# A new hand-over order for 1,900 pieces of an attention and gating kernel, with three more groups of idle products

## The chip, the cores and the metric

The kernel runs on one core of a Trainium2 chip. The metric is device time in microseconds (us), the median of several executions; lower is better. The engines are TensorE (PE in the rows, with its weight loads as PEld), VectorE (DVE), ScalarE (ACT), GpSimd (POOL) and SyncE (SP), which here only issues DMAs.

## The reference

Windowed attention with four sink keys, and behind it a gated feed-forward layer whose gate mixes positions:

```python
# q, k, v: (4, 8, 768, 64) f32; n_sink 4, window 128
scores = scale * np.matmul(q, k.transpose(0, 1, 3, 2))
keep = is_sink | in_window                     # 4 first keys, or the last 128
a = np.exp(scores - max); a = a / (sum + 1e-9)
x = (a @ v) as (4, 768, 512)
h = np.maximum(x @ w_in, 0.0)                  # w_in (512, 1024)
u, v = h[..., :512], h[..., 512:]
v_n = (v - mean) / np.sqrt(var + 1e-06)
v_s = np.einsum('ts,bsd->btd', w_spatial, v_n) + b_spatial[None, :, None]
return (u * v_s) @ w_out                       # (4, 768, 512)
```

## The kernel before

The work is cut into about 1,900 pieces. A batch b has six tiles t of 128 positions, and each tile two halves hf of four heads; the 48 halves are numbered 0 to 47. For one half there are these pieces:

- `scores`: products of queries and keys into banks `sc` (L882 in f32 in the first batch, L888 as three f16 products later). VectorE then adds the mask and takes the maximum (L893, out `pexp` and `nm`), ScalarE takes the exponential (L898).
- `weights`: `pexp` is split into a high and a low f16 part (`p`; high is L538 on ScalarE or L547 on GpSimd, low is L554 on VectorE or GpSimd), and SyncE issues two DMAs that transpose them into `pT` (L963). In the first three tiles of batch 0 TensorE transposes instead (`weights_whole`, L930 and L945 into `tr`), and ScalarE or VectorE copies `tr` to `pT` (L934, L948).
- `attend`: `pT` times values into `av` (L1001 to L1003 with the sinks in L995; in the first three tiles L1014 with the sinks in L1009). VectorE divides by the sum (L1021 to L1025), two engines split the result into `x`, and a DMA transposes it to `xT` (L1045).

Behind these stand the large products, all of them through `three` (L575), each a sum of three f16 products: `ps_v` (half v of `x @ w_in`, 12 products of 512 columns), `ps_u` (half u, 12 of 256), `ps_s` (the mix over positions, 18 of 256) and `ps_o` (the output, 12 of 512). Loading and splitting the weights (`decode`, L634 to L641, then L540 and L561) is also cut into pieces, which stand between those of the first batches. L638 is one of its steps on VectorE, and L561 the low part of a split.

There are few buffers: four banks `sc`, one double bank `av`, and two banks `mm` that `tr`, `ps_v`, `ps_u`, `ps_s`, `ps_o` and the idle products share.

What is emitted, and in which order, is one table of numbers, `ORDER`. A number is a piece by its rank; a letter behind it (a, d, p) names the engine where a piece may run on several. Each engine's queue is this table read from the start, so each engine runs its pieces in that order and waits where one's inputs or buffer are not there:

```python
    def order(self):
        self.prepare()
        todo = [(self.ps[int(x.rstrip("adp"))], x[-1]) for x in ORDER]
        todo = [(p, e if e in "adp" else p[2]) for p, e in todo]
        self.where = {p[1]: e for p, e in todo}
        for p, e in todo:
            yield p[4], e
```

A piece is registered with a time and a number `columns`, which describe it to whoever makes the table; `order` reads neither.

`keep_clock` (L1174) makes one group of idle products: four products of ones with 256 columns into a bank that nobody reads. `FILLERS` says how many such pieces exist; those that `ORDER` names are emitted. Before, it names six of 24.

Of the kernel before, what the change touches and what calls it, by code (L numbers as in the profile page):

```python
# [19 lines left out]
P = 128  # L20
# [247 lines left out]
FILLERS, FILLER = 24, 4  # L268
# [3 lines left out]
5 0 1895 1 3 2 4 1908 6 11 1898 10 53 1889 7 164 1894 9 14 13 8 42 39 15 44 16 43 51 41 40 50 62 46 47 45 63 37 1887 64 17 112 48 52 116 38 111 73 19  # L272
229 74 12 65 49 68 105 67a 21 72 20 18 69 83 66 82 22 387 54 71 75 70 88 86 91 55 85 87 25 26 104 89d 100 84 172 163 101 107 162 23 92 103 61 93 128
106 31 319 110 263 109 108 246 27 32 123 90 129 113 102 28 57 115a 132 459 114a 127 131 209 165 126 124a 194 141 156 142 140 143 33 130 29 146 125 34
150 159 222 151 139 158 183 221 94 154 145a 147 144a 133 166 152 148 182 153 96 169a 173 135 35 155 179 157 161 178 171 76 193 170a 36 160 188 30 95
223 185 168 192 186 199 97 197a 187 190 174a 191 205 24 215 206 175 184 58 230 207p 118 201 228 189 198 217 149 220 78 212p 98 200 210 243 196d 204
219 218 225 216 56 244 224 59 211 232 134 117 213 245a 226 257 119 208 250 77 252p 233 227 248 176 247 260 234a 259 276 251 240 136 231 275 239 253
262 167 261 267 120 291 235 283 137 271 277a 258 274 138 79 236 270 121 286 343 279 285 288 278 280 344 305 60 287 99 304 292 177 313 281d 346 294
306a 284 122 282 237 297 311p 300 309 299 318 315 307 80 316 293 317 328 327 351p 310 321 298 81 290 337 312 295a 352 289 379 349 323 417 416 353 339
453 329p 340 334 296 372 389 322 326 333p 331 241 342 314 341 302 371 301 330 336 375 350 373a 242 338 332 376 418 335 525 354 264 345 308 355 180  # L280
377p 374 423 424a 366 362 363 360 348 480 383 432 272p 378 385 361 356a 181 249 390 386 358 481 642 357 303 384 421 195 397 347 420 202p 393 394 214
414 320 203p 381 415 392 254 391 398a 422 410 412 238 411 400p 359 413 524 494 419 441a 426 273p 364 430 428a 533 429 365 367 255 475 324a 256 565 409
431 325p 368 438 437 493 577 388 600 265 439 443d 405 594 442 266 506 447 460 444 831 446 268 399 425 395a 448 621 396p 445 507 473a 512 427 531 625
369 497 513 720 269 370 676 440 454 502 727 532 449 488 433 539a 673 435 496 474p 450 582 434 504a 436 540p 689 505 456 461 458 451 541 500p 590 601
465 455 463 406 556 501 467 401 490 495 572 457 602 557 466 1023 603d 498 468 575 610a 573 476a 469 452 574d 464 477 478d 566p 470 492 658 402 462 479
611d 576 499 489 592a 753 471 491 548 593p 659 660d 482 671a 520a 672p 622 549 484 483 550p 825 522d 472 485 407 521 526 560a 563 503 623 562 523 624d
706 567 561p 635a 486 631 510 487 529 636p 637 732 707 509 708p 511 528 514 530 718p 515 686 516 568 380 733 719p 508 734d 517 527 534 745a 687 542a
564 640p 551 638 537 643 755 536 518 746p 905 559 543 688p 519 695a 781 682 554 756 696p 952 535 757d 546p 544 553 538 632 583 569 552 782 555 666 584
717 783d 408 604 854 585a 545 633 1395 587 578 570a 589p 586 760 579 403 580 767a 581 596 547 571 675 598 588 800p 597 612p 684 605 614 777 599 665
609 648 644 646p 607 591 641 613p 617 608 628 639 630 714 759 674 618 606 790 615a 404 683 558 627 647 629 595 1396 768d 663p 619d 649 721 616 626  # L290
669p 873 620 656 657 680 655 667 681 654 780 634 679 690 664 776 668 652 796p 650a 694 670 882 651 678 794 645 700p 699 791 691 692 702 713 834 693
864 870 715 703 704d 710 653 722 835 711 677 661 712 836p 740 747 735 729 662 705 797 738a 844p 728 709 795 701 749 742p 743 731 778 730 752 739 716
751 758 784 741 801d 798 750 744 811 871 764 1071 935 763 876 723a 874p 845d 926 789 779 799 770a 761 725 724 786 812 769 772 792 867 813p 855 773 762
822p 774d 726 802 748 788 787 807 824 736 771 816a 685 737 827 785 823d 775 833 872 818 820p 866 793 927 978 697a 809 803a 808 819 899 810 698p 821
804 837 888 875 889 933p 856 850 830 839 930 817 838 754 805 840 765p 841 829 928 846 828 861 847p 897 766d 860 1111 863 849p 877 806 826 862 814 1842
894p 859 858 883 815 931 885 951 886 991 896p 884 985 869 891 907 848 382 934 878a 865 997 960 911 895 909 1105 868 902 879 901 1029 903 898 908 880
904 932 925 915p 832 887 914 922 910 842a 958 917d 994 1060 881 843p 924 892 992 936 1006 893 921 923 943 1061 900 993 939 947a 918 941 906 995a 944
912p 942 956 948 949d 955 1069p 961 916 940 919 1066 945 1350 950 965 1067 946 1050 962 954 996 920 1336 957 959 1149 890 963 1054 966p 1072 964 981
929 913p 982 1102 1156 1068 937a 969p 1254 1011 938 984 967d 968 971 1118 998 1062 1019 1840 953 972 973d 975 983 1351 1070 1014p 1009 1016 851 1374
1007 1027 1010 970 980 1017 852 1008 1176 976 1051 988 1025 974 977p 1028 1026 989p 999d 1143 1015 1018p 1004 1330 1052 1146 1053d 990d 1064a 1219 986  # L300
853 1065p 1020 1046 1034 1000 1044a 857 1087 1393 1077 987 1005 1075p 1036 1037 1057 1048p 1038 1058 1024 1088 1089d 1184 1035 1100a 1012 1059 1101p
1056 1047 1076 1092a 1049 1001 1185 1150 1186d 1098p 1279 1045 1073 1078 1002 1096 1196a 1055 1003d 1182 1375 1197p 1086 1097 1030 1110 1083 1021p
1093 1085 1107 1022p 1084 1109 1063 1013 1099 1161 1031 1079a 1449 1032d 1043 1074 1039a 1108 1040d 1119 1162 1131 1129a 1080 1263 1163p 1121 1299
1128 1225p 1122 1123 1226 1174a 1140 1106 1264 1141 1227 1132 1120 1175p 1142 1138 1130 1265d 1838 1305 1033 1273p 1115 1133d 1041p 1139 1283 1223
1293 1274d 1169 1167a 1151 1042p 1116 1220 1145 1168 1094 1450 1117p 1170 1152a 1160 1171p 1134 1158 1124a 1157 1179 1153 1181 1328 1095 1159 1103
1144 1125p 1280 1173 1549 1224 1281 1303p 1178 1112 1359 1187 1104 1260 1180 1210 1198 1513 1191 1300 1228 1199p 1193 1387 1190 979 1218 1203p 1201
1177 1363 1192 1154 1211 1216 1212d 1217 1304 1329 1229p 1202 1221 1215 1204 1230p 1247 1214 1245a 1514 1302 1155 1222 1200 1249p 1366a 1165 1231
# [125 lines left out]
def fast_path(tc, st, scalars, qk, v, v0, vs, w_in, w_sp, w_rows, b_sp, b_col, w_out, out):  # L433
# [7 lines left out]
    with (  # L441
# [373 lines left out]
        def whole(b):  # L815
            return b < WHOLE
# [101 lines left out]
        def weights_whole(i, b, t, hf, r):  # L918

            n = n_blocks(t)  # L920
# [16 lines left out]
            if t > 1:  # L937
                k = n // 4
# [348 lines left out]
```

## Time and profile before

| what | us |
|---|---|
| three executions | 400.57, 401.19, 404.01 |
| median | 401.19 |
| the profiled execution, its own time | 399.68 |
| its span, first to last instruction | 397.9 |

The profile describes one execution. Its span is 1.8 us shorter than its time, and its time is 1.5 us under the median of the three. A row of the timeline gives the start, the duration, the engine, the line and the tiles (out<-in) of a run of like instructions; since products overlap in the pipeline, a run's duration reaches a little into the next one. The granted clock (PEclk) is 1.00 at TensorE's 2.4 GHz and 0.50 at 1.2 GHz.

### The profile page before, as it was taken

To read this page: it belongs to the slowest core of one execution; us is meant where nothing else is said; L and a number is where in the kernel's file an instruction comes from. 1 tells how busy PE (TensorE), PEld (TensorE's weight loads), DVE (VectorE), ACT (ScalarE), POOL (GpSimd) and SP (SyncE) were. 2 spreads that over 40 slices of the span, in tenths; PEclk is the share of its full clock that TensorE was granted. 3 is DMA by queue.
4 is the path that set the end of the run, shared out by engine and by line. 5 is a ranking of instruction groups with operands and counts; after the bars stand their busy time and mean duration, and the time that the engine had idled before them with its cause. 6 is when DMAs were issued, how large, how long until landed. Compare 5 with 4: busy or idle time off the path is not lost. (4 is left out here: it accounts for less than half of the span.)

```text
span 397.9 us, 10018 instructions
## 1 busy us (share of the span) xinstructions
PE 386.9 (97%) x3663; PEld 272.1 (68%) x3663; DVE 305.2 (77%) x900; ACT 280.3 (70%) x682; POOL 201.0 (51%) x262
## 2 busy tenths in 40 slices
PE   7998999989999999999999999999999999999995
PEld 5677477667856776567885765686778665678742
DVE  4898799898979998699899789787787757435520
ACT  4997799978988888879889867787775543322111
POOL 5236389665976657365859634634573022113010
PEclk9896899999999999999999999999999999999999
DMA  7998799987899998999999967968658984312003
GB/s 252 390 354 177 192 152 213 259 207 187 162 221 219 215 197 176 215 239 188 195 202 263 220 171 160 232 133 204 105 113 164 172 214 113 126 55 105 28 29 111
DMA packets 134872, 72.91 MB, mean 183 GB/s; under 512 B 114208, under 2 KB 118304, under 8 KB 134816
## 3 DMA queue, kind: packets, MB, share of 16 engines
q1 hardware_dynamic: 134400, 71.94, 79.1%
q8 instruction: 30, 0.49, 0.5%
q10 hardware_dynamic: 416, 0.26, 0.2%
q14 instruction: 26, 0.21, 0.2%
HBM read 38.17 MB, written 6.29 MB: 112 GB/s over the span
## 5 line engine op out<-in xcount | busy, mean ns | idle before, releaser
L575 PE MATMUL ps_s<-wsp,vn 128*128 128x256 f16 x864 | 99.1, 273 | 0.0
L898 ACT ACTIVATE pexp<-pexp,nm 128x260 f32<-128x260 f32 (+1 forms) x192 | 87.1, 486 | 13.0 <-DVE nm L893 12.5
L575 PEld LDWEIGHTS <-vn 128*128 128x128 f16 x864 | 83.1, 98 | 12.0 <-issue 1.7
L575 PE MATMUL ps_u<-xT,win 128*128 128x256 f16 x576 | 68.7, 273 | 0.1
L575 PE MATMUL ps_v<-win,xT 128*128 128x512 f16 x288 | 67.5, 386 | 0.1
L575 PE MATMUL ps_o<-wout,g 128*128 128x512 f16 x288 | 65.2, 379 | 0.4 <-DVE found L757 0.4
L575 PEld LDWEIGHTS <-win 128*128 128x128 f16 x576 | 54.9, 98 | 10.5 <-issue 1.2
L554 POOL TENSOR_TENSOR p<-pexp,p 128x1024 f16<-128x1024 f32 (+1 forms) x23 | 45.4, 1974 | 14.5 <-ACT p L538 13.9
L575 PEld LDWEIGHTS <-xT 128*128 128x128 f16 x288 | 27.8, 99 | 32.3 <-issue 3.1
L575 PEld LDWEIGHTS <-g 128*128 128x128 f16 x288 | 27.6, 98 | 32.2 <-issue 1.8
L554 DVE TENSOR_TENSOR p<-pexp,p 128x16 f16<-128x16 f32 (+2 forms) x49 | 31.4, 644 | 4.6 <-POOL p L547 3.0
L1165 ACT ACTIVATE ob<-ps_o 128x512 f32<-128x512 f32 x24 | 14.2, 592 | 28.9 <-PE ps_o L575 26.9
L1001 PE MATMUL av<-vring,pT 128*128 128x65 f16 x312 | 32.6, 193 | 1.3 <-DMA pT<-p 1.3
L538 ACT CAST p<-pexp 128x32 f16<-128x32 f32 (+2 forms) x54 | 29.6, 563 | 4.2 <-DMA pT<-p 4.0
L547 POOL TENSOR_SCALAR p<-pexp 128x1024 f16<-128x1024 f32 (+1 forms) x18 | 20.1, 1118 | 24.6 <-ACT pexp L898 9.0
L1002 PE MATMUL av<-vring,pT 128*128 128x65 f16 x312 | 32.5, 193 | 0.0
L1003 PE MATMUL av<-vring,pT 128*128 128x65 f16 x312 | 32.4, 193 | 0.1
L1001 PEld LDWEIGHTS <-pT 128*128 128x128 f16 x312 | 28.7, 97 | 3.1 <-DMA pT<-p 1.6
L554 POOL TENSOR_TENSOR g<-g,g 128x256 f16<-128x256 f32 x27 | 20.8, 772 | 18.9 <-ACT g L538 18.2
L1081 POOL TENSOR_SCALAR rs<-mv 128x1 f32<-128x1 f32 x24 | 8.6, 359 | 41.9 <-DVE mv L1074 39.5
L888 PE MATMUL sc<-kring,qp 64*128 64x260 f16 (+1 forms) x432 | 28.9, 262 | 0.6 <-DVE nm L893 0.5
L1139 DVE SCALAR_TENSOR_TENSOR ps_s<-ps_s,b_bc 128x256 f32<-128x256 f32 x35 | 15.1, 430 | 18.4 <-PE ps_s L575 17.1
(155 smaller groups left out, 766.7 us busy)
## 6 DMA issues: line engine op xcount, KB each, us to landing
qkraw<-qk_t SPq DMA_DIRECT2D x18, 512.0 KB, 4.4
out<-ob SPq DMA_DIRECT2D x24, 256.0 KB, 2.9
vraw<-v_s SPq DMA_DIRECT2D x21, 256.0 KB, 4.5
dec<-w_in SPq DMA_DIRECT2D x8, 512.0 KB, 7.0
wrow<-w_in SPq DMA_DIRECT2D x8, 512.0 KB, 3.9
wrow<-w_sp_rows SPq DMA_DIRECT2D x6, 384.0 KB, 3.8
dec<-w_out SPq DMA_DIRECT2D x4, 512.0 KB, 4.6
wrow<-w_out SPq DMA_DIRECT2D x4, 512.0 KB, 3.7
```

The lines of the kernel that those rows point to most:

```text
L538: nc.scalar.copy(o, x)
L547: nc.gpsimd.tensor_scalar(o, x, 1.0 if sc is None else sc, 1.0, op0=ALU.mult, op1=ALU.mult)
L554: eng[e].tensor_tensor(out=o, in0=x, in1=hi, op=ALU.subtract)
L575: nc.tensor.matmul(o, a, m, start=(i == 0), stop=(i == n - 1))
L888: nc.tensor.matmul(o, qp[rows, qi, hp, :], keys(kring[:, ki], rows), start=(m == 0), stop=(m == 2))
L898: nc.scalar.activation(po, po, AF.Exp, bias=nm()[:, h2 + q:h2 + q + 1], scale=-1.0)
L1001: nc.tensor.matmul(o[:, h], ph, vh, start=(t < 2 and j == 0), stop=False)
L1002: nc.tensor.matmul(o[:, h], ph, vl, start=False, stop=False)
L1003: nc.tensor.matmul(o[:, h], pl, vh, start=False, stop=(j == nb - 1 and (t < 2 or h == HH - 1)))
L1081: nc.gpsimd.tensor_scalar(rs, vals["mv", i][:, 1:2], 1e-6, VNS ** -2, op0=ALU.add, op1=ALU.mult)
L1139: nc.vector.scalar_tensor_tensor(out=sums_at(), in0=ps(), scalar=1.0 / (SP_SCALE * VNS), in1=b_bc[:, t0:t0 + TC], op0=ALU.mult, op1=ALU.add)
L1165: plan.add(r + WHEN["o copy"], "a", 0.5, lambda e: nc.scalar.activation(tl("ob", i), tl("ps_o", i), AF.Copy, scale=1.0 / (G_SCALE * OUT_SC ...
```

## The change

`ORDER` is a new table: the same pieces in another order, 133 of them on another engine (30 from GpSimd to ScalarE, 24 the other way; 38 from GpSimd to VectorE, 29 the other way; 12 between ScalarE and VectorE), and nine idle groups instead of six. `FILLERS` rises to 36. The numbers `columns` of the scores, the transposes, the attend products and the idle products are others; `order` does not read them. Nothing that is computed changes.

```diff
-FILLERS, FILLER = 24, 4
+FILLERS, FILLER = 36, 4
...
-5 0 1895 1 3 2 4 1908 6 11 1898 10 53 1889 7 164 1894 9 14 13 8 42 39 15 44 16 43 51 41 40 50 62 46 47 45 63 37 1887 64 17 112 48 52 116 38 111 73 19
...
+5 3 1904 1 0 2 4 1911 11 10 1890 53 6 1903 9 165 1893 8 13 14 1912 111 37 39 15 116 42 40 1909 16 41 45 43 44 46 62 50 47 51 63 164 229 17 49 112 68
...
-                     columns=n * (260 if t else 128) * (2 if whole(b) else 1.5))
+                     columns=n * (260 if t else 128) * (1.2 if whole(b) else 0.8))
...
-                plan.add(r, "PE", 0.44, turn, [("pexp", i, h) for h in hs], [("tr", (i, k))], columns=1024)
+                plan.add(r, "PE", 0.44, turn, [("pexp", i, h) for h in hs], [("tr", (i, k))], columns=1650)
...
-                         columns=4 * 65 * n + (520 if t > 1 else 0))
+                         columns=333 * n + (90 if t > 1 else 0))
...
-                         columns=195 * n + (195 if t > 1 else 0))
+                         columns=165 * n + (30 if t > 1 else 0))
...
-            plan.add(200.0, "PE", 0.01 + 0.108 * FILLER, f, [], [("idle", k)], columns=2 * P * FILLER)
+            plan.add(200.0, "PE", 0.01 + 0.108 * FILLER, f, [], [("idle", k)], columns=2.5 * P * FILLER)
```

Where the three added groups stand: before the first scores there are six instead of five; the one behind all four scores of the first tile now stands between their two halves; a new one stands behind the first two scores of the second tile's second half; and a new one stands between the two last f32 attend products. That last place is on TensorE, in the third tile of batch 0. Before (`sc` are scores of the fourth and fifth tile, `psink` the sink weights):

```order
L882 MATMUL sc<-wsp,qkraw 128x260 x2
L945 MATMUL tr<-ident,psink 16x128
L882 MATMUL sc<-wsp,qkraw 128x260 x2
L930 MATMUL tr<-ident,pexp 128x128 x4
L1009 MATMUL av<-vsraw,pT 128x260
L1014 MATMUL av<-vring,pT 128x65 x8
L1009 MATMUL av<-vsraw,pT 128x260
L1014 MATMUL av<-vring,pT 128x65 x8
L882 MATMUL sc<-wsp,qkraw 128x260 x4
```

Now (four pairs of a weight load and an idle product, of which one stands):

```order
L930 MATMUL tr<-ident,pexp 128x128 x4
L882 MATMUL sc<-wsp,qkraw 128x260 x4
L930 MATMUL tr<-ident,pexp 128x128 x4
L1009 MATMUL av<-vsraw,pT 128x260
L1014 MATMUL av<-vring,pT 128x65 x8
L1174 LDWEIGHTS any
L1174 MATMUL idle<-any 128x256
...
L1009 MATMUL av<-vsraw,pT 128x260
L1014 MATMUL av<-vring,pT 128x65 x8
L882 MATMUL sc<-wsp,qkraw 128x260 x4
```

The idle group came between the two attend products, and the sink transpose (L945) went ahead of the scores.

The second attend product there reads a `pT` that VectorE copies (L934). On VectorE, ahead of that copy, before (L893 is the mask, printed as ISA):

```order
L893 ISA nm 128x1
L638 SCALAR_TENSOR_TENSOR w_487<-dec,w_487 128x512
L893 ISA pexp,nm<-sc,m_odd 128x260
L893 ISA nm 128x1
L934 COPY pT<-tr 128x512
```

Now:

```order
L561 SCALAR_TENSOR_TENSOR vring<-vring 128x8x64
L554 TENSOR_TENSOR x_529<-av,x_529 128x512
L634 TENSOR_SCALAR w_547<-dec 128x512
L561 SCALAR_TENSOR_TENSOR win<-w_322,win 128x512
L561 SCALAR_TENSOR_TENSOR vring<-vraw,vring 128x8x64
L934 COPY pT<-tr 128x512
```

The weight step L638 and the masks ahead of the copy went behind it, and two low parts (L561) came ahead of it.

On SyncE's queue, the four transposes of batch 1's first tile (`p_0` is half 0, `p_1` half 1), which the attend products of that tile wait for. Before:

```order
L963 DMA_TRANSPOSE pT<-p_0_137 128x4x128
L569 DMA qkraw<-qk_t 128x2x512
L569 DMA vraw<-v_s 128x512
L569 DMA vsraw<-v_sink 96x260
L963 DMA_TRANSPOSE pT<-p_1_138 128x4x128
L569 DMA vraw<-v_s 128x512
L963 DMA_TRANSPOSE pT<-p_0_137 128x4x128
L963 DMA_TRANSPOSE pT<-p_1_138 128x4x128
```

Now:

```order
L963 DMA_TRANSPOSE pT<-p_0_137 128x4x128
L569 DMA qkraw<-qk_t 128x2x512
L963 DMA_TRANSPOSE pT<-p_1_138 128x4x128
L963 DMA_TRANSPOSE pT<-p_0_137 128x4x128
L963 DMA_TRANSPOSE pT<-p_1_138 128x4x128
```

Three loads that stood among the four went elsewhere.

## Rows read from the trace of the kernel before

**Rows 1.** The page: TensorE's busy share, and its clock in 40 slices.

```profile
PE 386.9 (97%) x3663; PEld 272.1 (68%) x3663; DVE 305.2 (77%) x900; ACT 280.3 (70%) x682; POOL 201.0 (51%) x262
PEclk9896899999999999999999999999999999999999
```

**Rows 2.** Busy time by stretch; last three columns PEclk, DMA share, GB/s.

```profile
9.20:12.50 3.30, 3.29 (x15) 2.12 (x14) 2.42 (x10) 3.24 (x11) 1.17 (x2) 0.50 1.01 350
12.60:32.90 20.30, 20.30 (x146) 14.95 (x144) 19.04 (x62) 18.91 (x43) 8.49 (x13) 1.00 0.98 351
33.10:43.20 10.10, 9.08 (x33) 5.92 (x34) 7.68 (x25) 8.63 (x18) 6.32 (x6) 0.50 0.86 166
43.30:90.90 47.60, 46.06 (x491) 32.64 (x490) 43.38 (x119) 41.26 (x105) 30.16 (x36) 1.00 0.97 207
90.90:393.20 302.30, 301.13 (x2945) 211.47 (x2942) 228.85 (x665) 203.69 (x500) 148.71 (x179) 1.00 0.77 167
```

**Rows 3.** Waits of TensorE: waited for, us in total, times, longest.

```profile
PE av L1001 <- DMA pT<-p: 1.3, 1, 1.3
PE av L1014 <- DVE pT L934: 1.2, 1, 1.2
PE sc L888 <- DVE nm L893: 0.5, 1, 0.5
```

**Rows 4.** Timeline of TensorE around 33 us.

```profile
30.31 2.00 PE L1014 MATMUL av<-vring,pT 128*128 128x65 f32 x16
32.24 0.70 PE L1009 MATMUL av<-vsraw,pT 16*128 16x260 f32 x2
34.12 3.68 PE L1014 MATMUL av<-vring,pT 128*128 128x65 f32 x16 [1.18 <-DVE pT L934]
37.73 2.10 PE L882 MATMUL sc<-wsp,qkraw 64*128 64x260 f32 x8
39.76 4.47 PE L575 MATMUL ps_v<-win,xT 128*128 128x512 f16 x12
44.17 1.15 PE L882 MATMUL sc<-wsp,qkraw 64*128 64x260 f32 x8
```

**Rows 5.** Timelines of VectorE and GpSimd at the same place.

```profile
30.60 2.52 DVE L638 SCALAR_TENSOR_TENSOR w<-dec,w 128x512 int32<-128x512 int32 x1
33.38 0.68 DVE L934 COPY pT<-tr 128x512 f32<-128x512 f32 x1
35.92 0.69 DVE L638 SCALAR_TENSOR_TENSOR w<-dec,w 128x512 int32<-128x512 int32 x1
...
30.51 2.05 POOL L554 TENSOR_TENSOR p<-pexp,p 128x1024 f16<-128x1024 f32 x1
```

**Rows 6.** Timeline of TensorE in the opening.

```profile
8.66 0.62 PE L1174 MATMUL idle<-any 128*128 128x256 bf16 x4
9.10 1.02 PE L930 MATMUL tr<-ident,pexp 128*128 128x128 f32 x4
10.14 2.10 PE L882 MATMUL sc<-wsp,qkraw 64*128 64x260 f32 x8
...
14.94 0.61 PE L930 MATMUL tr<-ident,pexp 128*128 128x128 f32 x4
```

**Rows 7.** Timelines of TensorE and SyncE at 72 to 80 us; a transpose's landing.

```profile
74.90 2.76 PE L575 MATMUL ps_v<-win,xT 128*128 128x512 f16 x12
78.91 0.84 PE L888 MATMUL sc<-kring,qp 64*128 64x260 f16 x12
...
72.31 1.21 SPq L963 DMA_TRANSPOSE pT<-p  x1
77.11 3.28 SPq L963 DMA_TRANSPOSE pT<-p  x2
...
DMA to landing us min/median/max: 4.7/5.3/5.5
```

More of the change, by code (lines that the diff above doesn't have):

```diff
@@ L276 @@
[L276 to L295, printed above, removed]
@@ new lines @@
+564 576 611p 658 510 491 482 494 592p 483 508 484 562 548 659 472 485 660d 406 631 511 671a 600 593d 520a 622 672d 495 407 521 522p 486 549 509 594
+550d 526 623 560a 515 624d 534 561p 523 583 635a 706 529 636p 538 527 905 567 530 642 528 487 584 555 686 544 637 707 514 708d 676 643 516 718p 638
+551 687 542a 517 688d 732 535 719d 543 568 536 546p 537 553 559 569 1395 518 695a 755 733 554 545 552 734p 580 547 696d 587 570a 745p 578 585a 519
+746p 958 781 756 598 586 579 596 589p 757d 640a 581 666 597 782 1396 588 404 599 591 783d 1105 604 408 767a 612p 854 605 615a 571 850 768p 760 682 609
@@ new lines @@
+994 944 1066 943 941 916 929 939 955 843p 954 1006 950 937d 893 956 938 1449 996 961 1182 940 948 987 1050 957 964 1067 969p 962 1146 963 919 945 971
+981 972 1068 946 1054 953 920 993 983 1149 970 982 906 965 912a 959 1102 984 973d 968 1156 1016 966a 913d 998 974 1118 967p 852 980 1014a 1010 1072
+1008 1011 1007 1069a 1015 1018p 988 1026 1176 975 1009 1028 1070 1393 1025 1336 1019 1330 1219 1034 1027 976 1017 999a 1004 977d 1020 1077 1035 1044p
+1036 1056 1038 1150 890 853 1075p 1000 1073 1037 1087 1043 1048d 1057 1058 1005 1076 1046 989a 1024 1047 1840 1088 990d 1089p 1051 1074 1023 1100p
@@ new lines @@
+1322 1410d 1421 1388 1373 1337 1435 1482 1409 1380 1418 1352 1606 1839 1444 1407 1381 1445 1286 1189 1343a 1453p 1394 1411 1353 1344p 1447 1516 1403a
+1446 1464 1404d 1457p 1455 1417 1465 1607 1466 1386 1467 1454 1206 1509 1473 1425 1608 1605 1521 1486p 1397 1456 1488 1602 1318 1609 1490p 1477 1658
+1476 1501 1459 1474 1436a 1424 1616 1500 1405 1519p 1587 1599 1475 1326 1437 1650 1498 1510 1499 1485 1726 1531 1588 1517 1589d 1540 1489 1841 1659
+1603p 1518 1296 1604p 1660 1532 1541 1533d 1536a 1512 1544p 1504 1545p 1412 1316 1520 1522 1413 1463 1414p 1529 1527 1557 1426p 1621 1530 1491 1555
@@ new lines @@
+1678 1645 1681 1767d 1590 1830 1772 1773 1769 1831 1774 1775 1770 1777 1591 1779d 1814 1778 1780d 1592 1791 1593 1822 1698 1800 1792 1748 1804 1699
+1700 1747 1757 1787 1756 1759 1870 1788 1789d 1793a 1794d 1875 1871 1872d 1873a 1874d 1865 1876 1877d 1878a 1879d 1854 1866 1867d 1868a 1869d 1801
+1855 1856d 1859a 1860d 1781 1802 1803d 1805a 1806d 1795 1782 1783d 1784p 1785p 1825 1796 1797d 1798a 1799d 1819 1826 1827d 1828p 1829d 1807 1820 1701
+1821p 1850 1823a 1832 1808 1824p 1809d 1812p 1813p 1810 1833 1834d 1851 1835a 1836d 1852 1815 1853 1881 1817 1760 1880 1883 1811 1882 1884 1885 1857
@@ L331 @@
+1816 1818 1858 1861 1863 1862 1864
 """.split()
```

79 lines of the change are left out of this document (41 added, 38 removed).

## The prediction

> **What bounds the kernel now.** I read the page first: TensorE is busy for 97% of the span, the other engines for 51 to 77% [rows 1]. The reader should see that no order can gain much by overlapping better; only three things can give: time in which TensorE waits, time in which it runs slow, and the ends of the program. The clock line of the same page shows where it runs slow: two dips in the first 45 us, then nothing below 9 tenths [rows 1]. The stretches by window tell the rest [rows 2]: the clock is 0.50 from 9.2 to 12.5 us and from 33.1 to 43.2 us, 1.00 in between and after 43.3. From 90.9 us to the end of the products, TensorE is busy 301.13 of 302.30 us, so nothing of size is left there. The waits by releaser agree [rows 3]: apart from the start, TensorE waits 1.3, 1.2 and 0.5 us at three places.
>
> The second dip is the dear one. TensorE waits 1.18 us at 33 us for a copy on VectorE, after a stretch of thin f32 attend products, and then runs at 1.2 GHz until 43.2 us [rows 4]. In that dip VectorE is busy 7.68 and ScalarE 8.63 of 10.10 us, so TensorE is what everything waits for. In the first dip ScalarE is busy 3.24 of 3.30 us [rows 2]: there the slow clock costs next to nothing.
>
> **The change part by part.** The numbers in `columns` reach nothing on the chip, since `order` does not read them; neither does a larger `FILLERS`. What changes is the table: an order, engines, and 12 more idle products. All sums are made against the profiled execution, 399.68 us.
>
> The clock from 33 to 43 us. The same work stands in the trace at both levels. Sixteen attend products take 3.68 us there and 2.00 just before; eight scores 2.10 and, at 44.17 us, 1.15 [rows 4]; twelve `ps_v` products 4.47 and, later, 2.76 [rows 4, 7]. If the clock holds, 1.68 + 0.95 + 1.71 = 4.34 us go. Will it hold? Before the fall came thin products and a wait. Now four dense idle products stand in just that place, and the wait should shrink (next paragraph). The same thin products ran at 1.00 from 12.6 to 32.9 us with nothing between them but scores and transposes [rows 2]. I take it that it holds, at 2 in 3; the bounds are 0 and 4.34.
>
> The wait of 1.18 us. It ends with the copy L934 at 33.38 us, which was late because the weight step ahead of it on VectorE took 2.52 us where its sister took 0.69; GpSimd's subtraction ran from 30.51 to 32.56 in the same time [rows 5]. Now that step stands behind the copy. But two low parts stand ahead of it, which also read two tiles, and the same subtraction comes on GpSimd when ScalarE has made the high part; that cast moved from GpSimd to ScalarE, just ahead of ScalarE's own transpose copy. If the low parts run first, the wait goes; if one meets the subtraction, it loses up to 2.52 − 0.69 = 1.8 us again. Between 0 and 1.8 us of wait I take 0.3, as the last low part needs a cast that ScalarE runs ahead of the one that frees the subtraction: −0.9 us.
>
> The Trainium skill (SBUF — State Buffer, section on two separate sides) says that a VectorE operation with two SBUF inputs and a GpSimd operation that reads SBUF take a shared port pair as an exclusive lock: whoever starts first keeps it for its whole instruction. The 2.52 us in this trace agree with it. By that rule it is the start order of the last low part and the subtraction that decides, which is the first rival below.
>
> The idle groups. One takes 0.44 us of the queue in the trace, from its start at 8.66 us to the next start at 9.10 [rows 6]. The sixth one ahead of the first scores lies in the wait for the first data. The one in the second tile lies in a stretch where ScalarE sets the pace (18.91 of 20.30 us busy, [rows 2]): at most 0.5, I take 0.1. The one between the attend products lies in the wait if there is one, else on the path: 0 to 0.5, I take 0.4. Together +0.5. Without cover it is +1.1.
>
> The first dip. Transposes took 1.02 and scores 2.10 there against 0.61 and 1.15 [rows 4, 6], 1.4 us. With ScalarE at 98% of that stretch I count it at 0 (bounds 0 and −1.4).
>
> The wait at 81 us, 1.3 us [rows 3]. `av` of batch 1 waits for a transposed `p`. The third and fourth transposes were issued at 77.11 us, 4.8 us behind the first, and land some 5.3 us later [rows 7]. Now three of the four loads between them are gone. Twelve scores (0.84 us, [rows 7]) that stood in front of the wait went further ahead, so TensorE also comes earlier. Bounds 0 and −1.3; I take −0.6.
>
> The feeders. If TensorE gains some 5 us at 33 to 43 us, VectorE and ScalarE must deliver everything after that so much earlier. From 33.1 to 90.9 us VectorE is busy 7.68 + 43.38 of 57.7 us, idle 6.6; ScalarE 8.63 + 41.26, idle 7.8 [rows 2]. Gains of 5.5 us would leave VectorE 1 us idle in 52, a share of 98%, and ScalarE would need 96%. VectorE reached 94% from 12.6 to 32.9 us (19.04 of 20.30), so I expect part of it back: 0 to +3.5, I take +1.5. What hides it is that the table puts other `ps_u` products ahead there.
>
> Engines. 133 pieces move, net 15 away from GpSimd, mostly high parts to ScalarE. Nothing after 90.9 us waits for them, since TensorE is never short there [rows 2]; the 0.5 us wait of a score [rows 3] may go or turn up elsewhere: 0. The order of large products among themselves costs nothing: each kind takes the same wherever it stands, and scores are entered from another kind as often as before.
>
> Sum: −4.3 − 0.9 + 0.5 − 0.6 + 1.5 = −3.8, or 395.9 us in a profiled execution. The three executions had their median 1.5 us above that one. I carry half of it over, since some of that spread will be dips and waits like these that differ from run to run: **396.6 us**, 1.1% under 401.19.
>
> **The rivals.** (1) *The clock falls all the same.* A low part of VectorE starts behind GpSimd's subtraction, the copy is late by up to 1.8 us again, and four idle products are not enough to bridge that. For it: two such operations stand there now. Against: their order, and 0.45 us of dense products. Then the 4.34 and 0.9 stay, the idle groups and part of the wait at 81 us remain: 399.7 + 1.1 − 0.6, with half the spread 400.9. No difference that can be measured. (2) *It holds, but the feeders become the bound.* The clock is won and TensorE waits for masks and exponentials until it is back at the old schedule: the gain shrinks by the whole +3.5 instead of 1.5, to 398.6. For it: the shares of 98% and 96% that they would need. Against: the products put ahead. (3) *Slower: TensorE catches up with its feeders and the clock falls at new places.* TensorE arrives 4 to 5 us earlier at pieces whose inputs come no earlier. One wait of 1.2 us with the fall behind it cost 1.18 + 4.34 = 5.5 us [rows 4]; the wait of 1.3 us at 81 us cost no clock (1.00 in its stretch, [rows 2, 3]). From waits somewhat beyond that on, two such falls while the first dip stays cured give 396.6 + 11 = 407.6; one gives 402.1, still within 1%. Against: after 90.9 us one microsecond of waiting is all there is now. (4) *It does not do what it says:* the weights act on nothing here, so if the place of the idle group is wrong, the table is just another order of equal work: that is rival 1.
>
> **How the numbers follow.** The forecast (394 to 398) has a chance of 0.48, rival 1 with 4 has 0.24, rival 2 has 0.16, rival 3 has 0.12, a third of it with one fall only. About 1%, 4 us, is what a measurement of this kernel can tell from no change (the three executions span 3.4 us). Faster by more than that: the forecast without its upper edge, and nothing else, 0.47. Slower by more: rival 3 with two falls, and some of its single falls in a bad place, 0.11. The rest, 0.42, lies within. The range goes from 393.0, where the 4.34, 1.18 and 1.3 all go, the idle groups cost 0.5 and nothing is given back (399.68 − 6.3, rounded down), to 402.5, above rivals 1 and 2 and a single fall.
>
> **What would show it.** Right: PEclk 1.00 from about 30 to 45 us; L1014's last sixteen products near 2.0 us, the `ps_v` behind them near 2.8 us; the first `ps_v` starting near 36 us instead of 39.76; a wait under 0.5 us ahead of the second idle place; VectorE's busy share between 45 and 85 us well above 91%. Wrong: a slice with the clock at 0.50 behind 30 us; a L561 of over 2 us right ahead of L934; a list of TensorE's waits with new rows on masks or `pT` of over 1 us. The prediction fails most easily at the 2-in-3 for the clock, and at the half spread between profiled and median execution.

## The result and the profile of the changed kernel

The changed kernel takes **397.96 us** in the median of 19 executions (396.12 to 400.54); the kernel before took 401.95 beside it (398.78 to 404.77). As measured, the ratio is 0.9896, with a 95% interval of 0.9872 to 0.9919 (the quotient of these medians is 0.9901). In a second comparison (the fifth experiment) it was 0.9960, 0.9920 to 0.9999. It is faster in both, by 0.4 to 1%, in the second only just. The two intervals do not overlap although the kernel is the same, so from one comparison to another a ratio can move by 0.006 without a cause in the kernel. The forecast was 396.6, in a range of 393.0 to 402.5, which takes in no change as well. The profiled execution took 397.38 us (span 395.6) against 399.68 of before. Of the two profiled executions, that of before lies 2.3 us under its median and that of the changed kernel 0.6 under its own, so the traces show 1.7 us less of a difference than the medians.

The page of the changed kernel, TensorE's busy share and its clock, as in [rows 1]; below it the stretches of [rows 2], in the same columns:

```profile
PE 382.9 (97%) x3675; PEld 270.0 (68%) x3675; DVE 310.2 (78%) x907; ACT 282.8 (71%) x690; POOL 191.8 (48%) x247
PEclk9999999999999999999999999999999999999999
```

```profile
9.20:12.50 3.30, 3.30 (x27) 2.29 (x26) 3.30 (x16) 3.30 (x10) 0.00 (x0) 1.00 1.05 374
12.60:32.90 20.30, 19.32 (x142) 14.57 (x140) 18.35 (x63) 19.65 (x46) 8.84 (x11) 1.00 1.08 331
33.10:43.20 10.10, 10.10 (x57) 5.58 (x57) 9.42 (x29) 8.56 (x19) 6.59 (x5) 1.00 1.15 210
43.30:90.90 47.60, 44.26 (x476) 31.59 (x476) 45.28 (x118) 42.04 (x107) 33.96 (x38) 1.00 0.97 215
90.90:391.00 300.10, 297.41 (x2931) 210.07 (x2927) 229.94 (x664) 204.25 (x503) 136.59 (x164) 1.00 0.75 166
```

Both dips are gone: the clock is 1.00 from 9.2 to 12.5 us and from 33.1 to 43.2 us, where it was 0.50. But TensorE, which was busy 46.06 of 47.6 us from 43.3 to 90.9 us, is now busy 44.26, and behind 90.9 us it is idle 2.7 instead of 1.2 us. TensorE's timeline at the place of [rows 4]:

```profile
29.36 2.00 PE L1014 MATMUL av<-vring,pT 128*128 128x65 f32 x16
31.20 0.60 PE L1174 MATMUL idle<-any 128*128 128x256 bf16 x4
31.73 0.70 PE L1009 MATMUL av<-vsraw,pT 16*128 16x260 f32 x2
32.36 2.00 PE L1014 MATMUL av<-vring,pT 128*128 128x65 f32 x16
34.29 1.15 PE L882 MATMUL sc<-wsp,qkraw 64*128 64x260 f32 x8
35.37 2.76 PE L575 MATMUL ps_v<-win,xT 128*128 128x512 f16 x12
```

No wait stands ahead of the second attend, and all three kinds run at the fast durations; the first `ps_v` starts at 35.37 instead of 39.76 us. On VectorE the two low parts ahead of the copy L934 took 0.68 us each and the copy started at 30.07 us:

```profile
28.87 0.68 DVE L561 SCALAR_TENSOR_TENSOR win<-w,win 128x512 f16<-128x512 f32 x1
29.47 0.68 DVE L561 SCALAR_TENSOR_TENSOR vring<-vraw,vring 128x512 f16<-128x512 f32 x1
30.07 0.68 DVE L934 COPY pT<-tr 128x512 f32<-128x512 f32 x1
```

TensorE's waits, as in [rows 3], have new rows instead:

```profile
PE ps_v L575 <- ACT wsp L540: 2.2, 1, 2.2
PE ps_s L575 <- ACT u L1115: 0.9, 1, 0.9
PE av L995 <- DVE x L554: 0.9, 2, 0.6
PE ps_u L575 <- ACT u L1115: 0.5, 1, 0.5
```

**Lost time.** To compare two orders, take a piece's start on TensorE and subtract the ordinary durations of all pieces ahead of it (the median spacing behind 95 us, shape by shape: `ps_v` and `ps_o` 2.60, `ps_s` 1.97, `ps_u` 1.31, scores 0.77 and attends 0.84, both less in the first tiles of a batch, idle groups 0.45; for the f32 kinds of the opening, the shortest seen of the same shape). What remains was lost so far, to waits and to the slow clock. The ordinary durations sum to 370.0 us before and 371.4 in the changed kernel, which has three idle groups more.

| lost by (us) | 15 | 30 | 45 | 90 | 130 | 300 | last `ps_o` |
|---|---|---|---|---|---|---|---|
| before | 7.2 | 9.6 | 15.6 | 18.3 | 18.8 | 22.7 | 23.0 |
| changed | 4.8 | 7.8 | 9.2 | 14.1 | 14.7 | 19.7 | 19.8 |
| difference | -2.4 | -1.8 | -6.4 | -4.2 | -4.1 | -3.0 | -3.2 |

A lead of 6.4 us at 45 us; 2.2 us of it are given back by 90 us and 1.0 us behind that. With 1.3 us more of work the last `ps_o` starts 1.8 us earlier (388.57 instead of 390.41).

### The profile page after: what moved, and what is told of

It reads as the page before. It is cut to its first block, busy times and chain, and to the rows that moved or that the text cites. A ratio compares the mean times of both kernels' runs of the same rounds, so it can differ in the third digit from the quotient of the medians.

```text
span 395.6 us, 10039 instructions
## 1 busy us (share of the span) xinstructions
PE 382.9 (97%) x3675; PEld 270.0 (68%) x3675; DVE 310.2 (78%) x907; ACT 282.8 (71%) x690; POOL 191.8 (48%) x247
## 4 chain that ended last, share of the span: by engine, by line
PE 71%; DMA 9%; DVE 8%; ACT 4%; issue 3%; POOL 2%; SPq 2%; ACTq 0%; POOLq 0%; DVEq 0%
PE ps_s L575 23%; PE ps_o L575 14%; PE ps_u L575 10%; PE ps_v L575 9%; PE sc L888 5%; DMA pT<-p 3%; DMA wsp<-qk_t 2%; PE av L1001 2%; PE av L1002 2%; PE av L1003 2%; PE sc L882 2%; DVE pexp L893 2%; DMA qkraw<-qk_t 1%; DVE vr L1090 1%; DMA xT<-x 1%
## 5 line engine op out<-in xcount | busy, mean ns | idle before, releaser
L575 PE MATMUL ps_v<-win,xT 128*128 128x512 f16 x288 | 65.9, 380 | 3.0 <-ACT wsp L540 2.2
L554 POOL TENSOR_TENSOR p<-pexp,p 128x1024 f16<-128x1024 f32 (+1 forms) x26 | 51.2, 1970 | 10.1 <-ACT p L538 9.3
L575 PEld LDWEIGHTS <-xT 128*128 128x128 f16 x288 | 27.0, 98 | 35.4 <-DMA xT<-x 3.6
L538 ACT CAST g<-g 128x256 f16<-128x256 f32 x30 | 12.0, 400 | 35.1 <-DVE g L1143 28.4
L1139 DVE SCALAR_TENSOR_TENSOR ps_s<-ps_s,b_bc 128x256 f32<-128x256 f32 x41 | 17.6, 429 | 18.4 <-PE ps_s L575 18.2
L554 DVE TENSOR_TENSOR p<-pexp,p 128x16 f16<-128x16 f32 (+2 forms) x46 | 29.2, 644 | 0.8 <-ACT p L538 0.8
L1001 PEld LDWEIGHTS <-pT 128*128 128x128 f16 x312 | 28.8, 97 | 1.4 <-issue 0.6
L1002 PEld LDWEIGHTS <-pT 128*128 128x128 f16 x312 | 28.6, 97 | 0.7
L1003 PEld LDWEIGHTS <-pT 128*128 128x128 f16 x312 | 28.5, 97 | 0.0
L1165 ACT ACTIVATE ob<-ps_o 128x512 f32<-128x512 f32 x24 | 14.2, 590 | 19.7 <-PE ps_o L575 19.6
```

What stands on the lines that cost most here:

```text
L538: nc.scalar.copy(o, x)
L554: eng[e].tensor_tensor(out=o, in0=x, in1=hi, op=ALU.subtract)
L575: nc.tensor.matmul(o, a, m, start=(i == 0), stop=(i == n - 1))
L1001: nc.tensor.matmul(o[:, h], ph, vh, start=(t < 2 and j == 0), stop=False)
L1002: nc.tensor.matmul(o[:, h], ph, vl, start=False, stop=False)
L1003: nc.tensor.matmul(o[:, h], pl, vh, start=False, stop=(j == nb - 1 and (t < 2 or h == HH - 1)))
```

## The experiments

All but the fifth edit the table, so each diff is a fragment of `ORDER`, with unchanged numbers around it. The kernel before ran beside each. The last column counts executions with a low mean granted clock over the span: at most 0.991 where the opening is that of before (before, e1, e2, e7, e9, e12), at most 0.994 where it is the changed one or has the sixth group. The first dip alone, 3.3 us at 0.50 in 397, leaves 0.996; either bound thus means some 4 to 5 us at half clock beside it. All 106 executions of before that ran beside the experiments are that low (0.975 to 0.991), and 5 of 19 of the changed kernel.

The count is coarse, as the mean doesn't tell which stretch was slow. Of the traces, those with the fall at 33 us and no first dip on record (e3, e6, e12) have a mean of 0.989 to 0.991, those with one fall elsewhere (e5 at 73 us, e7 at 126, e10 at 90) 0.994 or 0.995. The first dip, too, is not in every trace of the old opening: e7's hasn't got it. And in e12's the record has the clock at 1.00 there, though the opening's transposes took 1.06 us, the slow duration, so a dip can be missing from the record.

| experiment | median | ratio to before, 95% | lost by 45, 90, 130, 300 us | low clock |
|---|---|---|---|---|
| e1 before + idle group | 399.52 | 0.9989 (0.9956 to 1.0023) | 12.9, 16.0, 16.9, 21.0 | 8 of 12 |
| e2 before, copy first | 397.63 | 0.9928 (0.9889 to 0.9967) | 10.9, 14.1, 16.9, 21.6 | 2 of 9 |
| e3 changed - idle group | 399.49 | 0.9973 (0.9943 to 1.0003) | 11.7, 17.8, 19.2, 23.9 | 9 of 12 |
| e4 changed - two groups | 400.01 | 0.9987 (0.9953 to 1.0021) | 10.1, 16.1, 16.7, 23.4 | 1 of 12 |
| e5 changed again | 398.68 | 0.9960 (0.9920 to 0.9999) | 8.6, 14.5, 15.1, 19.4 | 4 of 12 |
| e6 e2 + sixth group | 397.17 | 0.9937 (0.9908 to 0.9967) | 12.9, 15.9, 18.6, 23.3 | 4 of 11 |
| e7 e2, loads behind | 398.70 | 0.9981 (0.9949 to 1.0014) | 10.0, 12.6, 15.4, 21.2 | 8 of 12 |
| e8 changed, divide first | 400.15 | 1.0014 (0.9981 to 1.0047) | 8.6, 15.1, 17.4, 22.3 | 1 of 12 |
| e9 e2, low part first | 395.93 | 0.9889 (0.9833 to 0.9945) | 10.8, 13.7, 14.3, 19.5 | 1 of 6 |
| e10 changed, copies first | 397.58 | 0.9930 (0.9891 to 0.9969) | 9.4, 15.8, 18.0, 21.3 | 2 of 12 |
| e11 joined | 399.44 | 0.9991 (0.9947 to 1.0034) | 9.4, 14.7, 15.6, 19.1 | 4 of 12 |
| e12 e9, loads behind | 395.78 | 0.9888 (0.9856 to 0.9920) | 14.6, 16.3, 16.9, 21.5 | 6 of 12 |

### What holds the clock at 33 us: e1, e2, e3

e1 puts an idle group (1905) between the attend products 189 and 216 of before:

```diff
-228 189 198 217
+228 189 1905 198 217
```

> The kernel before with one group of four idle products more, between the two last f32 attends; nothing else moves, so VectorE's late copy stays. Theory A (the dense idle products are what keeps the clock): granted clock 1.00 from 33 to 43 us, the last sixteen attend products 2.0 us, the twelve ps_v behind them 2.8 us; the wait ahead of the attend shrinks from 1.18 to about 0.7 us. That wins 4.3 us at 43 us; some of it is given back by 90 us as in the changed kernel, so about 398.5 to 400 us against the median of before near 402. Theory B (the wait is what lets the clock fall; idle products are too short to bridge it): the clock stays at 0.50 there, the time stays within 0.5 us of before.

e2 moves VectorE's weight step (78) behind the copy (196):

```diff
-149 220 78 212p 98 200 210 243 196d 204
+149 220 212p 98 200 210 243 196d 78 204
```

> The kernel before with one piece moved: VectorE's weight step L638 stands behind the copy L934 instead of ahead of it and of one mask. No idle products are added. Theory B (the wait decides): the wait of 1.18 us goes, the clock holds at 1.00 through 33 to 43 us, 5.5 us are won there and part of them is given back by 90 us: about 398 to 400 us. Theory A (only dense products hold the clock behind the thin f32 attends): the wait goes, the clock still falls, at most 1.2 us are won: about 401 us.

e3 takes the group out of the changed kernel:

```diff
-196d 134 1905 217 208
+196d 134 217 208
```

> The changed kernel without the idle group between the two last f32 attends; its order keeps the copy early. Theory A: the clock falls to 0.50 from about 32 us on, sixteen attends take 3.7 us and ps_v 4.5 us, 4.3 us are lost at 43 us and with what the feeders gave back before about 2 remain: about 400 us. Theory B: the clock holds, 0.4 us fewer on the path: 397.5 to 398 us, no difference from the changed kernel.

TensorE's timeline of e1, then e2, then e3 (the last sixteen attends, eight scores, the first `ps_v`):

```profile
34.58 2.39 PE L1014 MATMUL av<-vring,pT 128*128 128x65 f32 x16 [0.76 <-DVE pT L934]
36.90 2.10 PE L882 MATMUL sc<-wsp,qkraw 64*128 64x260 f32 x8
38.94 2.99 PE L575 MATMUL ps_v<-win,xT 128*128 128x512 f16 x12
```

```profile
32.94 2.00 PE L1014 MATMUL av<-vring,pT 128*128 128x65 f32 x16
34.87 1.15 PE L882 MATMUL sc<-wsp,qkraw 64*128 64x260 f32 x8
35.95 2.76 PE L575 MATMUL ps_v<-win,xT 128*128 128x512 f16 x12
```

```profile
32.08 3.12 PE L1014 MATMUL av<-vring,pT 128*128 128x65 f32 x16
35.13 2.10 PE L882 MATMUL sc<-wsp,qkraw 64*128 64x260 f32 x8
37.17 3.92 PE L575 MATMUL ps_v<-win,xT 128*128 128x512 f16 x12
```

Neither theory A nor B stands alone. With the idle group and a wait of 0.76 us (e1) the clock still falls, later and for a shorter time. Without the group and without a wait it holds in e2 and falls in e3. One trace is one draw: with the copy early and no group at that place, the traces of e2, e7 and e9 hold and those of e3, e6 and e12 fall; with both, all six hold (the changed kernel, e4, e5, e8, e10, e11). Over executions, the order of before with the copy early and no group at that place (e2, e6, e7, e9, e12) has the low clock in 21 of 50, with the group and the wait left (e1) in 8 of 12, where before has it always; the changed order without the group (e3) in 9 of 12, with it (the changed kernel, e4, e5, e8, e10, e11) in 17 of 79. With one bound for all, 0.991, the four shares are 21 of 50, 8 of 12, 4 of 12 and 5 of 79; with 0.994 they are 31 of 50, 8 of 12, 9 of 12 and 17 of 79. So the early copy takes the low clock from always to about half, and in the changed order, where the copy is early anyway, it is the group that makes it rarer: on one chip, e3 has it in 9 of 12 and e4, which keeps the group, in 1 of 12. (Of the 17, some have it behind the wait at 72 us, as e5 below.)

The Trainium skill (TensorE: Matmul & The Clock Gate, Part 1 on the clock gate) says that the window over which the clock gate judges runs freely and doesn't start with the kernel, so that the same kernel has a different number of slow products from run to run. The page says it of the rise at a kernel's start. A fall that comes in one execution and not in another would fit it; no run here sets that phase.

### The opening: e4, e6

e4 takes the groups 1909 (between the first score halves) and 1888 (second tile) out of the changed kernel:

```diff
-42 40 1909 16 41
+42 40 16 41
...
-19 89a 1888 86 54
+19 89a 86 54
```

> The changed kernel without two idle groups of the opening, the one between the score halves of the first tile and the one behind the first scores of the second tile's second half. The changed kernel is 2.4 us of work ahead of before at 15 us, at a clock of 1.00 where before has 0.50 from 9.2 to 12.5 us. Theory C (these idle groups hold the clock there, and the slow clock was on the path): the dip comes back, TensorE is 1.4 us or more later at 15 us, about 399 us. Theory D (the order brought it; ScalarE sets the pace there, so the clock is worth nothing): the first attend starts no later, time within 0.5 us of the changed kernel, with or without a dip.

e6 is e2 with a sixth group ahead of the first scores:

```diff
-164 1894 9 14
+164 1894 1891 9 14
```

> The kernel before with the copy ahead of the weight step (as in the second experiment) and a sixth idle group ahead of the first scores, as the changed kernel has. Theory E (the first dip comes from TensorE's pause before the first scores, which the sixth group fills): clock 1.00 from 9 to 12.5 us as well; if the slow clock was on the path there, another 1 to 2 us are won against the second experiment, about 396 us; if ScalarE hides it, nothing, 397.6. Theory D (the order of the opening removes the dip, not the idle group): the dip stays, 397.6 us.

The stretch of the first dip in e4 and in e6, in the columns of [rows 2]:

```profile
9.20:12.50 3.30, 3.30 (x25) 2.32 (x24) 3.30 (x16) 3.30 (x11) 0.00 (x0) 1.00 1.00 344
```

```profile
9.20:12.50 3.30, 2.76 (x20) 1.86 (x20) 2.97 (x13) 3.30 (x11) 1.30 (x3) 1.00 0.98 294
```

The clock is 1.00 in both. So the two groups are not needed for it. That the sixth group cures the dip in the order of before (theory E) fits e6, where the wait ahead of the first scores is 0.45 us against 1.06 in e2, but it isn't shown. e7 (below) has no sixth group and waits 0.91 us there, and its clock is 1.00 as well; e4 waits 1.03 us without a dip. e7's stretch, and its first transposes at the fast duration:

```profile
9.20:12.50 3.30, 2.76 (x20) 1.84 (x20) 3.09 (x13) 3.30 (x11) 1.20 (x2) 1.00 1.03 363
9.03 0.60 PE L930 MATMUL tr<-ident,pexp 128*128 128x128 f32 x4
```

What the dip costs lies between nothing and 0.9 us: the second attend product starts at 15.03 us in e6 and 14.52 in e7, against 15.46 in e2 and 15.38 before. By the last pair of attend products e6 has lost its lead again (32.33 us, e2 32.31), e7 has kept 0.9 us (31.37). In the changed kernel the second attend product starts at 13.40 and in e4 at 13.24, so most of the 2 us there come from the order. By the last pair most of that has gone again (31.73 against 32.24).

e6's trace also has the fall at 33 us, with no wait ahead:

```profile
32.96 3.52 PE L1014 MATMUL av<-vring,pT 128*128 128x65 f32 x16
```

That e4's median is 400.01 is not explained by the opening: at 31.7 us its trace agrees with the changed kernel's within 0.03 us, and it loses 1.2 us at 86 (0.3 in the changed kernel), 1.0 at 190 (none there) and 2.3 at 262 us (1.8). Its interval overlaps that of e5, and why it is no faster than before stays open.

### Where the lead is given back, first place: e5, e8

e5 is the changed kernel unedited, for a second trace.

> The changed kernel itself, unedited, for a comparison beside the others and a second profiled execution. Ratio to before between 0.987 and 0.993; the same fixed waits of its order as in the first profile: some 2.2 us ahead of ps_v at 72 us, 0.9 us ahead of ps_s at 262 us. If those are accidents of one execution, they are absent here.

Its TensorE at 70 us, beside that of the first trace (which is the second fence):

```profile
69.74 1.47 PE L575 MATMUL ps_u<-xT,win 128*128 128x256 f16 x12
73.66 4.26 PE L575 MATMUL ps_v<-win,xT 128*128 128x512 f16 x12 [2.45 <-DMA xT<-x]
```

```profile
70.67 1.47 PE L575 MATMUL ps_u<-xT,win 128*128 128x256 f16 x12
74.36 2.76 PE L575 MATMUL ps_v<-win,xT 128*128 128x512 f16 x12 [2.21 <-ACT wsp L540]
```

The wait is no accident; the ratio, 0.9960, is above the 0.987 to 0.993 that were expected. The trace of e5 names what the wait is for: the DMA transpose of `x`, which the changed kernel's first trace issues at 69.47 us; nothing that `ps_v` reads comes from `wsp`. In e5 the clock fell behind the wait: 4.26 instead of 2.76 us. In e3, where TensorE comes 3.5 us later, the wait is the same 2.2 us. So it isn't TensorE's lead that makes it, but the chain from the attends over division, split and transpose, and what the order leaves to cover it.

e8 shortens that chain: the division (419) ahead of a mask and a normalisation, a weight's low part (367) behind the low part of `x`.

```diff
-238 394 320
+238 419 394 320
...
-359 419 413 415 367 427
+359 413 415 427
...
-430 429 400d
+430 429 367 400d
```

> The changed kernel with two moves on VectorE near 66 us: the division of the sixth tile stands ahead of a mask and a normalisation, and its low part ahead of a weight step. Theory F (the 2.4 us wait ahead of the last ps_v of the first batch is the length of a chain from the attend products over division, split and a DMA transpose that the new order gives too little work to cover): the transpose is issued about 1 us earlier and the wait shrinks by as much, to 1.2 to 1.5 us; 0.5 to 1 us less than the changed kernel if it isn't given back. Theory G (the engines that feed are simply full, so any lead is given back): the wait shrinks there and comes back within 20 us, no change of the time.

The transpose went out at 68.21 us, 3.2 us behind the end of the attends instead of 3.8, and the wait shrank by only 0.2 to 0.4 us (2.0 in the list of waits). The kernel was not faster: 400.15 against 398.68 of e5 on the same chip. VectorE's timeline of e8 shows why a shorter chain was no gain, in two of the weights' low parts:

```profile
68.10 1.79 DVE L561 SCALAR_TENSOR_TENSOR wsp<-wraw,wsp 128x768 f16<-128x768 f32 x1
72.98 1.91 DVE L561 SCALAR_TENSOR_TENSOR wsp<-wsp 128x768 f16<-128x768 f32 x1
```

In the changed kernel they took 0.95 us each. Moved by a microsecond, they now meet GpSimd's operations, as L638 did in [rows 5]. Summed over VectorE's instructions from 45 to 90 us, each against its shortest duration in the traces of this order, e8 loses 4.5 us to such stretching, e5 0.6. Theory F has the chain right. What was won is gone by 91 us, where e8 has new waits (0.7 and 1.4 us ahead of `ps_u`, 1.6 ahead of a `ps_v`); that the new meetings make these waits is likely, not shown.

### Second place, and the order behind 90 us: e7, e9, e12, e10, e11

e7 is e2 with three loads (600, 405, 831) behind batch 1's four transposes:

```diff
-577 388 600 265 439 443d 405 594 442
+577 388 265 439 443d 594 442
...
-444 831 446
+444 446
...
-396p 445 507
+396p 445 600 405 831 507
```

> The kernel before with the copy ahead of the weight step and, on the DMA queue, three loads moved behind the four transposes of batch 1's first tile, as the changed kernel has them. The wait of 1.3 us of av at 81 us then goes or shrinks to under 0.4; 1.0 us less than the second experiment at 90 us. If the loads decide, about 396.7 us; if the transpose is late for another reason (its own low part comes late), the wait stays at 1.2 us or more, 397.6 us.

The wait of `av` at 75 to 80 us, 1.4 us in e2, is gone (0.8 us turn up ahead of a `ps_s` at 80 us), and e7 is 1.5 us ahead of e2 at 90 us (12.6 against 14.1 lost). But 0.9 us of that stand at 45 us already, ahead of the loads' place, since its trace lacks the first dip; what the loads won is 0.6 us. By 130 us it has lost 2.8 us more. The time, 398.70, is no gain over e2's 397.63, where 396.7 was expected, and 8 of the 12 executions have the low clock. All three kernels e2, e6 and e7 lose over 2 us at the same two pieces there, the scores and the `ps_v` at 121 to 128 us; before loses nothing. VectorE and GpSimd in e2:

```profile
121.72 3.07 DVE L554 TENSOR_TENSOR p<-pexp,p 128x1024 f16<-128x1024 f32 x1
```

```profile
121.61 2.10 POOL L554 TENSOR_TENSOR p<-pexp,p 128x1024 f16<-128x1024 f32 x1
```

VectorE's low part starts 0.11 us behind GpSimd's and takes 3.07 us (3.08 in e6 and e7, 1.22 in before), and four masks stand behind it, for which the scores' banks wait. By the rule of the Trainium skill in the prediction (SBUF — State Buffer, two separate sides) the first to start keeps the ports for its whole instruction. From the rows that makes 2.10 - 0.11 + 1.22 = 3.2 us, an estimate; the trace agrees within 0.15. In e7 the clock also fell behind these waits, in the `ps_v` (4.33 us instead of 2.76):

```profile
125.89 4.33 PE L575 MATMUL ps_v<-win,xT 128*128 128x512 f16 x12 [0.42 <-ACT ob L1165]
```

e9 is e2 with a low part of a gate (768) moved behind those masks, so that VectorE's low part comes first:

```diff
-595 1396 768d 663p 619d
+595 1396 663p 619d
...
-681 654 780 634
+681 654 768d 780 634
```

> The second experiment's kernel (before, copy ahead of the weight step) with one more move on VectorE: the low part of a gate g stands behind the four masks of the fifth tile instead of ahead of the low part of a p, so that this low part starts some 1.2 us earlier, ahead of GpSimd's low part and not 0.11 us behind it. Theory H (what gives the lead back at 121 to 128 us is that VectorE's low part runs behind GpSimd's: 3.07 us instead of 1.22): it takes 1.2 to 1.3 us, the waits of 1.15 us ahead of the scores and 1.18 us ahead of ps_v there go, about 2 us less than the second experiment in the trace; near 395.6 to 396.5 us. Theory G (VectorE is full in any case): the low part is short, the waits stay above 1.5 us in sum, 397.6 us.

```profile
120.11 1.22 DVE L554 TENSOR_TENSOR p<-pexp,p 128x1024 f16<-128x1024 f32 x1
```

```profile
120.33 1.90 POOL L547 TENSOR_SCALAR p<-pexp 128x1024 f16<-128x1024 f32 x1 [2.90 <-ACT pexp L898]
122.31 2.06 POOL L554 TENSOR_TENSOR p<-pexp,p 128x1024 f16<-128x1024 f32 x1
```

In the trace it goes as theory H says: 1.22 us, no wait at either piece, 0.6 us lost from 90 to 130 us instead of 2.8; the time is 395.93 us. The price moved to GpSimd's cast (1.90 instead of 1.04 us in e2), for which nobody waits. But the move also took the gate's low part (1.29 us in e2) out from ahead of the masks, and the two shares aren't separated: in e12, with the same move, the low part met the cast and took 2.06 us, and no wait came back. Nor is the gain in time over e2 shown by itself, as the intervals overlap. Two moves on VectorE alone, with no idle product more, do about as much against before as the new table (0.9889 to its 0.9896 and 0.9960; the two weren't run side by side).

e12 adds the three loads of e7 to e9 (the fragments are those of e7).

> The ninth experiment's kernel (two moves on VectorE) with the three loads of the seventh behind the four transposes. The seventh took the wait of 1.3 us at 75 to 80 us away in its trace, but lost its lead at 121 us, where VectorE's low part met GpSimd's. With that meeting gone, theory H expects the second gain to show in the time: the wait ahead of av under 0.3 us, no wait over 0.5 us from 118 to 130 us, about 395 us, 0.5 to 1 us below the ninth. Theory G (whatever is won early is lost by 130 us): no change against the ninth, or slower, 396 us or more.

The wait of `av` is 0.3 us at most and none over 0.5 stands at 118 to 130 us, as theory H said, but the time is that of e9 (395.78), where 0.5 to 1 us less was expected. Its profiled execution is one in which the clock fell at 34 us with no wait ahead:

```profile
34.17 3.53 PE L1014 MATMUL av<-vring,pT 128*128 128x65 f32 x16
37.63 2.10 PE L882 MATMUL sc<-wsp,qkraw 64*128 64x260 f32 x8
39.67 3.50 PE L575 MATMUL ps_v<-win,xT 128*128 128x512 f16 x12
```

Of its twelve executions the six with a clock above 0.991 have a median of 394.8 us, the other six 397.2. So 2.4 us go with the low clock; that the second dip makes all of it isn't shown, as only one of the twelve was traced. The next step would be e12 with the idle group of the changed kernel; it wasn't run.

e10 puts two of ScalarE's `u` copies (1397, 1616) of the changed kernel ahead of measuring steps (1608, 1602):

```diff
-1473 1425 1608 1605
+1473 1425 1397 1608 1605
...
-1488 1602 1318
+1488 1616 1602 1318
```

> The changed kernel with two of ScalarE's copies of ps_u put earlier in its queue near 260 us, each ahead of one measuring step of 0.8 to 1.3 us. Theory I (the 0.9 and 1.1 us that TensorE waits there in each execution of the new order are banks that a copy behind a measuring step frees late): both waits fall under 0.3 us, 1.5 us less than the changed kernel at 300 us, near 397 us where the changed kernel had 398.7. If other work would be late next, the waits turn up within the next 10 us and the time stays.

The two waits at 260 us (0.5 and 0.9 in the list above, 0.7 and 0.9 in e5) are gone and 0.5 us stands behind them; from 130 to 300 us this order now loses 3.3 us, 5.0 and 4.3 in the two traces of the changed kernel. (At 90 us, far from the edit, its trace has a wait of 2.1 us ahead of a `ps_v` and the clock falls behind it, 4.39 us instead of 2.76.) Theory I is right about the place. The time, 397.58, fits it, but e5 ran on another chip and the intervals overlap, so the gain in time isn't shown.

e11 takes the changed table up to piece 313 (44 us), and behind it all that is left in the order of before, with before's engines.

> The changed kernel's order as far as the scores of the sixth tile at 44 us (with all nine idle groups), and behind that the order of before, with its engines. If the change wins what it wins in the first 45 us and its order behind that only costs (2.4 us ahead of ps_v at 72 us, 1.9 us at 260 us), this is faster than the changed kernel by 1 to 2 us: about 396.5 to 397.5. If the order behind 45 us is no worse in itself and the lead is what is given back, about 398.7 us as the changed kernel; VectorE's low part may meet GpSimd's at 121 us as in the second experiment, 2.3 us.

That failed: 399.44 us. It loses 5.3 us from 45 to 90 us, as much as the changed kernel (4.9): new waits of 0.7 and 0.5 us at the seam, 2.1 us at the `av` of batch 1. From 90 to 300 us it loses 4.4, the changed kernel 5.6, and 1.4 us more at the end, where a `ps_o` waits for the flag. So it can't be said that the change's order behind 45 us is what costs.

## Why the prediction was right, point by point

The mechanism was right: the clock holds at 33 to 43 us. The size was met in part by luck. The traces moved by 2.3 us, where the sum said 3.8; the medians moved by 4.0, because the profiled execution of before was a fast one of its kind. And within the sum errors of both signs cancelled.

- **Clock (-4.34) and wait (-1.18, taken as -0.9).** Right: 2.00, 1.15 and 2.76 us, no wait, `ps_v` at 35.37 where "near 36" was forecast. The reason given was dense idle products *and* a shorter wait: with both, none of six traces has the fall at 33 us, with the early copy alone three of six, with the group alone (e1) it came. The chance of 2 in 3 was low for both together (the low clock came in 17 of 79), about right for the wait alone.
- **Idle groups (+0.5).** The sixth lies in the first wait, as said (0.24 us of it remain, 0.98 before). The two that e4 takes out cost nothing by 31.7 us. The one between the attends lies on the path: 0.45.
- **First dip (0).** Between nothing (e6) and 0.9 us (e7), so 0 may be low. What was missed is the order in the same stretch: the second attend product starts 2 us earlier, of which 0.5 remains at 32 us.
- **Wait at 81 us (-0.6).** It is gone, and e7 shows that the three loads made it. But 0.8 us turn up right behind it there, and what e7 wins against e2 from 45 to 90 us is 0.6, the size that was taken (e12 against e9: 1.2).
- **Feeders (+1.5).** The step that was mis-sized, and for another reason than given. TensorE's waits from 45 to 90 us sum to 4.1 us in the changed kernel (0.63, 0.46, 0.25, 2.38, 0.34) and 1.8 before (0.31, 1.5); without the wait at 81 us that is +3.7, beyond the bound of 3.5, and some 1 us more is lost between 38 and 45 us. VectorE went to 95% (45.28 of 47.60), as forecast; but the largest wait is a chain that ends in a DMA transpose and is there whether TensorE comes early or late (e3).
- **Behind 90 us (0).** Wrong: +1.0 by lost time. "Nothing after 90.9 us waits for them" was true of the order of before and taken over to the new one; at 260 us ScalarE's `u` copies stand behind measuring steps (e10).
- **Profile and median.** Half the spread (+0.75) was carried over; the medians moved 4.0 us where the traces moved 2.3.

Counted by starts, the changed kernel is 6.1 us ahead at the end of the first `ps_v`, 5.0 at 45 us, 2.8 at 90 and 1.8 at the last `ps_o`.

Rival 1 described the right meeting of VectorE and GpSimd at a place where it didn't happen (L561 took 0.68 us); it happened at 121 us in e2, e6 and e7. Rival 2 was right that part of the gain comes back by 90 us. Of rival 3, a fall behind a new wait, e5 has one (1.5 us at 74 us), and so has e10 (1.7 at 90).

## What to carry to other kernels

Where TensorE runs thin products and then waits, cure the wait first: moving one instruction of the late engine behind the awaited copy gave about what a new order of the whole program gave (0.9928 in e2, against 0.9896 and 0.9960), and in the changed order dense idle products then made rarer what was left. A lead won early can be lost where a VectorE and a GpSimd operation come to start at the same moment, as at 121 us in e2, e6 and e7: after each move, look for an instruction that takes longer than its sisters, and change which of the two starts first. Judge a chance event such as a fall of the clock by the mean clock of many executions, not by one trace.

## What the runs showed of the hardware

- The same instruction of VectorE with two SBUF inputs took 1.22 us ahead of GpSimd's cast, 2.06 in e12 (where GpSimd's cast had started 0.05 us before), and 3.07 behind GpSimd's low part; GpSimd's cast behind it took 1.90 instead of 1.04. A shift of some 0.1 us in which of the two starts first moves one to two microseconds from one engine to the other.
- The clock fell to 0.50 with no wait ahead on TensorE, within the last sixteen thin f32 attend products (3.12 us in e3, 3.52 in e6, 3.53 in e12, instead of 2.00). Other traces of the same order there (e2, e7, e9) do not have the fall.
- Executions of one program spread by 3 to 8 us; in e12 some 2.4 us of it go with the clock.
